# A new order for the second half of a hand-ordered RWKV + FFN kernel, and the last output tile copied out of two PSUM banks

## The chip, the cores and the metric

The kernel runs on one core of one Trainium2 chip. The metric is the device time of one execution in microseconds; lower is better. Each kernel is timed in several runs, and one execution of it is also profiled. The five engines of a core take their instructions in program order, each from its own queue, and wait for each other through semaphores: PE (TensorE, matmuls), DVE (VectorE), ACT (ScalarE), POOL (GpSimd) and SP (SyncE, here only a queue that issues DMAs). Matmuls write PSUM, which has eight banks; DVE and ACT read it from there.

## The reference

A recurrence over 768 tokens for 4 x 8 heads of 48, and behind it a feed-forward block on the 3072 x 384 result:

```python
for t in range(S):
    cur = np.einsum('bhd,bhe->bhde', u[None] * kt, vt)
    y[:, :, t] = np.einsum('bhd,bhde->bhe', rt, state + cur)
    state = wt[:, :, :, None] * state + np.einsum('bhd,bhe->bhde', kt, vt)
...
a = x @ w1
b = x @ w2
h = a * b @ w3
return (h @ w_out).astype(np.float32)
```

x is y with heads side by side (384 columns), d_ff is 1024. Inputs and output are float32.

## The kernel before

The sequence is cut into six chunks of 128 tokens, and chunk and batch into 13 units (`UNITS`): unit t covers one or two batches of one chunk. Units 0 and 1 have one batch, the others two. The state is carried from chunk to chunk; units of the same batches follow each other at a distance of two (5, 7, 9, 11 and 6, 8, 10, 12).

For each unit t the recurrence is written as matmuls. `ln_t` (ACT, L421) takes the logarithm of w, `cs_t` (PE, L437 and L442) sums it up over the tokens into two banks, and ACT reads those banks three times: `pc_t` (L449), `ne_t` (L454, exp of minus the sum) and `e_t` (L495). `iw_t`, `rw_t` (L491), `KRr_t` (L499) and `KRk_t` (L458) scale r and k; `dtr_t` and `dtk_t` (SP, L504 and L519) or `trk_t` with the copy `trke_t` (L529) transpose them. `m_t_b` (PE, L564) is the 128 x 128 product of r and k for batch b, and it is masked either by `msk_t_b` on DVE (L583) or by the copy `mcp_t_b` on ACT (L570) and the masking `maff_t_b` on POOL or DVE. `ys_t` (L599) and `yi_t_b` (L609) sum the output, `rk_t` (L533), `ruk_t` (L537), `dg_t` (L543) and `dv_t` (L552) make the term with u, and `yb_t` (DVE, L627) adds both and so frees the two banks of y. `dty_t_b` (SP, L636) or `yt_t` with `xT_t` transposes the result. `kv_t` (L680, L673), `T_t` (L687, L690), `S_t` (L702) and `Sb_t` (L707) carry the state on.

The feed-forward block of a unit has four groups g: `a_t_g` and `b_t_g` (PE, L727, six matmuls of 128 x 256 each) fill a bank each, `asb_t_g` (ACT, L732) copies a out, `abT_t_g` (DVE, L737) multiplies it with b. `o_t_b` (PE, L748, eight matmuls) multiplies with w34, the product of w3 and w_out that the first half makes (`wt`, `w3Te`, `wm`, `w34e`); `osb_t_b` (L753) copies the 128 x 384 result to one of four buffers, `st_t_b` (L757) stores it. The very last tile, unit 11 batch 0 (`LAST`), is done in two halves of 192 columns, `o_11_0` and `oh_11_0`, each with its own copy and store.

Nothing is scheduled by a compiler. `ORDER` is a list of step@engine in the order of the program; each engine takes its own steps in this order. `BANKS` gives each step its PSUM bank (`y7=3,4`, `cs10=3,4`), its copy of `a_sb` (`sa`), its mask buffer (`M`) and its output buffer (`so`). A step waits for the steps whose data it reads and for the last readers of the bank and buffer that it writes. So with `y7=3,4` and `cs10=3,4` the matmuls of `cs_10` wait until `yb_7` has read the sums of unit 7. No step that reads PSUM is given to POOL.

Of the kernel before, what the change touches and what calls it, by code (L numbers as in the profile page):

```python
# [67 lines left out]
vin_2@POOL warm0@21 cs_0@PE csT_0@PE ne_0@ACT vc_0@ACT KRk_0@DVE w1_1@POOL et_0@ACT ruk_0@DVE warm3@3 trk_0@PE
padet@DVE warm3@3 kv_0@PE trke_0@DVE pc_0@ACT mask@POOL trw_0@PE S_0@DVE KRw_0@DVE ln_2@ACT dg_0@DVE warm3@2 m_0_0@PE
w3_0@POOL Sb_0@ACT msk_0_0@DVE cs_2@PE dv_0@POOL csT_2@PE ne_2@ACT rin_1@POOL yi_0_0@PE et_2@ACT trw_2@PE KRk_2@DVE  # L70
yb_0@DVE w2_1@POOL trk_2@PE ln_1@ACT KRw_2@DVE yt_0@PE trke_2@ACT cs_1@PE w1_0@POOL rk_2@DVE csT_1@PE vin_1@POOL
ruk_2@DVE pc_2@ACT pc_1@ACT ne_1@ACT m_2_0@PE m_2_1@PE dg_2@DVE mcp_2_0@ACT KRk_1@POOL msk_2_1@DVE et_1@ACT
maff_2_0@POOL warm1@4 kv_2@PE xT_0@ACT trk_1@PE trke_1@ACT w2_0@POOL dv_2@DVE yi_2_0@PE yi_2_1@PE win_3@POOL yb_2@DVE
warm7@2 wt_1_0@PE wt_1_1@PE a_0_1@PE wo@POOL w3Te_1@ACT trw_1@PE yt_2@PE asb_0_1@ACT w3_1@POOL KRw_1@DVE wt_0_0@PE
wt_0_1@PE xT_2@DVE m_1_0@PE w3Te_0@DVE kin_3@POOL a_2_2@PE msk_1_0@DVE b_2_2@PE rin_3@POOL asb_2_2@ACT b_0_1@PE
S_2@DVE rk_1@DVE a_2_3@PE abT_0_1@DVE ruk_1@POOL a_0_0@PE abT_2_2@DVE a_2_0@PE dg_1@DVE a_2_1@PE dv_1@POOL asb_2_0@ACT
yi_1_0@PE b_2_0@PE asb_2_1@ACT w3_2@POOL yb_1@DVE kv_1@PE b_2_1@PE w3_3@POOL ln_3@ACT b_2_3@PE win_4@POOL abT_2_1@DVE
asb_2_3@ACT yt_1@PE b_0_0@PE asb_0_0@ACT xT_1@DVE S_1@DVE vin_3@POOL a_1_1@PE abT_2_0@DVE b_1_0@PE abT_2_3@DVE
asb_1_1@ACT b_1_1@PE abT_0_0@DVE cs_3@PE csT_3@PE win_5@POOL ne_3@ACT wm_0@PE et_3@ACT a_1_0@PE pc_3@ACT w34e_0@ACT
wm_1@PE kin_4@POOL asb_1_0@ACT abT_1_0@DVE wt_2_0@PE rin_4@POOL wt_3_0@PE KRk_3@DVE wt_2_1@PE wt_3_1@PE w3Te_2@DVE  # L80
trk_3@PE w3Te_3@ACT abT_1_1@DVE trw_3@PE vin_4@POOL trke_3@ACT Sb_1@DVE wm_2@PE KRw_3@DVE w34e_1@ACT m_3_0@PE
w34e_2@DVE m_3_1@PE wm_3@PE rin_5@POOL msk_3_0@DVE mcp_3_1@ACT maff_3_1@DVE ys_3@PE wt_5_0@PE w34e_3@DVE wt_4_0@PE
wt_4_1@PE kin_5@POOL wt_6_0@PE w3Te_4@DVE wt_6_1@PE wt_5_1@PE wt_7_0@PE w3Te_5@DVE wt_7_1@PE wm_4@PE ln_4@ACT
win_6@POOL rk_3@DVE ruk_3@DVE wm_5@PE w34e_4@ACT dg_3@DVE rin_6@POOL w3Te_6@ACT yi_3_0@PE iw_4@ACT w3Te_7@DVE
yi_3_1@PE cs_4@PE dv_3@DVE kin_6@POOL wm_7@PE e_4@ACT Sb_2@DVE yb_3@DVE ne_4@ACT pc_4@ACT KRk_4@DVE wm_6@PE win_8@POOL
ln_5@ACT yt_3@PE w34e_5@ACT rw_4@DVE trk_4@PE win_9@POOL xT_3@ACT KRr_4@DVE cs_5@PE w34e_7@DVE w34e_6@ACT trr_4@PE
pc_5@ACT trke_4@DVE ne_5@ACT kv_3@PE kv_4@PE T_3@DVE iw_5@ACT o_0_0@PE trre_4@DVE e_5@ACT T_4@DVE m_4_0@PE S_4@POOL
osb_0_0@ACT ys_4@PE msk_4_0@DVE m_4_1@PE st_0_0@SP o_1_0@PE S_3@POOL msk_4_1@DVE win_7@POOL a_3_1@PE ln_6@ACT a_3_2@PE
rk_4@DVE vin_6@POOL asb_3_1@ACT ruk_4@DVE yi_4_0@PE Sb_3@ACT cs_6@PE KRk_5@DVE b_3_1@PE asb_3_2@ACT vin_5@POOL
dg_4@DVE ne_6@ACT csT_6@PE yi_4_1@PE abT_3_1@DVE osb_1_0@ACT trk_5@PE rin_7@POOL et_6@ACT rw_5@DVE a_3_0@PE KRr_5@DVE  # L90
a_3_3@PE trke_5@ACT rin_9@POOL dv_4@DVE b_3_3@PE asb_3_3@ACT KRk_6@DVE trr_5@PE kin_7@POOL pc_6@ACT yb_4@DVE b_3_0@PE
trre_5@ACT trk_6@PE rin_10@POOL rk_6@DVE yt_4@PE abT_3_3@DVE trke_6@ACT b_3_2@PE rin_8@POOL o_2_1@PE xT_4@ACT
abT_3_2@DVE rk_5@DVE asb_3_0@ACT kin_8@POOL m_5_1@PE abT_3_0@DVE m_5_0@PE mcp_5_1@ACT trw_6@PE ruk_5@DVE o_3_1@PE
KRw_6@DVE osb_2_1@ACT maff_5_1@POOL msk_5_0@DVE o_2_0@PE osb_3_1@ACT ruk_6@POOL Sb_4@ACT dg_5@DVE st_3_1@SP m_6_1@PE
osb_2_0@ACT m_6_0@PE msk_6_1@DVE kv_6@PE ln_7@ACT T_6@DVE dv_5@POOL kv_5@PE a_4_2@PE ln_8@ACT b_4_2@PE msk_6_0@DVE
iw_7@ACT vin_8@POOL win_12@POOL o_3_0@PE asb_4_2@ACT T_5@DVE iw_8@ACT vin_7@POOL dg_6@DVE ys_6@PE ys_5@PE yi_5_0@PE
S_5@DVE yi_6_0@PE yi_5_1@PE a_4_1@PE yb_5@DVE yi_6_1@PE dv_6@POOL b_4_1@PE asb_4_1@ACT abT_4_2@DVE osb_3_0@ACT cs_7@PE
abT_4_1@DVE yt_5@PE rw_7@POOL e_7@ACT yb_6@DVE a_4_0@PE b_4_3@PE pc_7@ACT xT_5@DVE asb_4_0@ACT dty_6_0@SP cs_8@PE
ne_7@ACT kin_10@POOL b_4_0@PE ne_8@ACT st_3_0@SP KRk_7@DVE a_4_3@PE KRr_7@DVE e_8@ACT a_5_2@PE KRk_8@DVE dtr_7@SP
ln_9@ACT rk_8@DVE b_5_2@PE ruk_8@POOL b_5_0@PE dty_6_1@SP asb_5_2@ACT pc_8@ACT asb_4_3@ACT a_5_0@PE iw_9@ACT  # L100
abT_5_2@DVE abT_4_3@DVE a_5_1@PE win_10@SP S_6@POOL a_5_3@PE asb_5_0@ACT kin_9@POOL rw_8@DVE asb_5_1@ACT trk_7@PE
abT_4_0@DVE kv_7@PE trke_7@ACT rk_7@DVE b_5_3@PE vin_9@POOL KRr_8@DVE o_4_0@PE Sb_6@ACT Sb_5@ACT abT_5_0@DVE T_7@DVE
asb_5_3@ACT b_5_1@PE S_7@POOL osb_4_0@ACT abT_5_3@DVE m_7_0@PE st_4_0@SP ys_7@PE ruk_7@POOL mcp_7_0@ACT m_7_1@PE
abT_5_1@DVE st_2_1@SP kv_8@PE msk_7_1@DVE st_2_0@SP a_6_2@PE dtk_8@SP cs_9@PE maff_7_0@POOL dg_7@DVE b_6_0@PE ne_9@ACT
dtr_8@SP T_8@DVE a_6_0@PE asb_6_2@ACT KRk_9@DVE e_9@ACT yi_7_0@PE a_6_3@PE rw_9@DVE dtk_9@SP dv_7@DVE asb_6_0@ACT
yi_7_1@PE o_4_1@PE ln_10@ACT rk_10@DVE win_11@SP yb_7@DVE KRr_9@POOL o_5_0@PE osb_4_1@ACT dg_8@DVE Sb_7@ACT pc_9@ACT
asb_6_3@ACT cs_10@PE rk_9@DVE dtr_9@SP yt_7@PE ruk_9@POOL e_10@ACT o_5_1@PE xT_7@DVE st_4_1@SP osb_5_0@DVE pc_10@ACT
# [30 lines left out]
def kernel(  # L138
# [572 lines left out]
    def block(t):  # L711
# [27 lines left out]
        for b in range(nb):  # L739
            row = (b0 + b) * S + c * C  # L740
            parts = 2 if (t, b) == LAST else 1
            for z, mark in enumerate(("", "h")[:parts]):
# [3 lines left out]
                def _(eng, b=b, cols=cols):  # L746
                    for fi in range(FI):
                        nc.tensor.matmul(one(f"o{t}_{b}")[:, cols], lhsT=ab[:, fi, b * C:(b + 1) * C],  # L748
                                         rhs=w34[:, fi, cols], start=(fi == 0), stop=(fi == FI - 1))
# [57 lines left out]
```

## Time and profile before

| | us |
|---|---|
| median of the runs | 164.16 (163.75, 164.16, 164.83) |
| the profiled execution | 163.85 |
| its span, first to last instruction | 162.1 |
| mean granted TensorE clock | 0.997 |

Busy times in the profile are of instructions at work; the time in a semaphore wait is idle, and the view names what ended it. A row of the timeline merges neighbouring instructions of one line; the time of such a piece on a busy PE is best read from its start to the start of the next row, since the ends of matmuls overlap with what follows. On DVE the next instruction of a queue starts about 0.08 us before the end of the one ahead.

### The profile page before, as it was taken

How to read it: one execution, taken by the hardware profiler on the slowest of the kernel's cores; microseconds unless marked ns; L12 is line 12 of the kernel's file. 1: busy time of each engine (PE TensorE's matmuls, PEld its weight loads, DVE VectorE, ACT ScalarE, POOL GpSimd, SP SyncE). 2: the span in 40 equal slices, each digit the busy share in tenths (PEclk: the TensorE clock that was granted, in tenths of full speed). 3: DMA queues.
4: the chain of work that ended last, by engine and by line, in shares of the span. 5: the costliest groups of instructions: out<-in, count | busy, mean ns of one | idle time of the engine just before them, and what ended most of it. 6: DMA issues, size and time to landing. Idle time of an engine off the chain costs nothing.

```text
span 162.1 us, 4606 instructions
## 1 busy us (share of the span) xinstructions
...
## 2 busy tenths in 40 slices
...
GB/s 111 222 159 180 196 195 242 209 170 215 219 155 161 177 259 167 137 120 172 147 186 169 230 202 195 94 142 132 184 174 182 201 28 146 28 121 97 6 146 97
DMA packets 103718, 25.83 MB, mean 159 GB/s; under 512 B 95825, under 2 KB 101713, under 8 KB 103697
## 3 DMA queue, kind: packets, MB, share of 16 engines
...
q10 hardware_dynamic: 144, 0.10, 0.2%
q14 instruction: 7, 0.05, 0.1%
...
## 4 chain that ended last, share of the span: by engine, by line
PE 62%; DMA 20%; POOL 6%; DVE 6%; issue 2%; SPq 1%; ACT 0%; DVEq 0%; POOLq 0%
PE banks L727 31%; PE banks L748 18%; DMA rin<-in_r_dram 9%; DMA w_bf<-in_moe_w_dram 8%; DMA u_f<-in_u_dram 4%; PE banks L564 3%; PE banks L609 2%; PE banks L437 1%; PE banks L680 1%; PE banks L599 1%; PE banks L525 1%; POOL w_bf L358 1%; DVE dg L543 1%; POOL win L343 1%; POOL kin L343 1%
## 5 line engine op out<-in xcount | busy, mean ns | idle before, releaser
L727 PE MATMUL banks<-xT,w_bf 128*128 128x256 bf16 (+1 forms) x624 | 68.6, 264 | 0.0
L727 PEld LDWEIGHTS <-w_bf 128*128 128x128 bf16 x624 | 55.5, 98 | 7.0
L737 DVE TENSOR_TENSOR abT<-a_sb,banks 128x512 bf16<-128x512 f32 x48 | 31.9, 683 | 17.1 <-ACT a_sb L732 9.6
L732 ACT COPY a_sb<-banks 128x512 f32<-128x512 f32 x48 | 27.6, 591 | 21.5 <-PE banks L727 14.7
L748 PE MATMUL banks<-w,abT 128*128 128x384 bf16 (+1 forms) x200 | 33.9, 320 | 0.0
L748 PEld LDWEIGHTS <-abT 128*128 128x128 bf16 x200 | 18.8, 98 | 10.4
L583 DVE TENSOR_TENSOR Mbf<-banks,mask 128x1024 bf16<-128x1024 f32 x14 | 16.9, 1216 | 0.8 <-PE banks L564 0.6
L753 ACT COPY osb<-banks 128x384 f32<-128x384 f32 (+1 forms) x18 | 8.5, 471 | 13.6 <-PE banks L748 11.8
L421 ACT ACTIVATE lw<-win 128x768 bf16<-128x768 f32 (+1 forms) x13 | 10.3, 799 | 10.3 <-DMA win<-in_w_dram 10.3
L343 POOL DMA_DIRECT2D win<-in_w_dram x11 | 12.5, 1140 | 2.8 <-DMA wo_bf<-in_moe_w_out_dram 1.3
L537 POOL TENSOR_TENSOR ruk<-rk,u_bc 128x768 bf16<-128x768 bf16 (+1 forms) x7 | 10.8, 1537 | 4.9 <-DVE rk L533 4.4
L627 DVE TENSOR_TENSOR yb<-banks,dv 128x768 bf16<-128x768 f32 (+1 forms) x13 | 11.6, 892 | 2.4 <-PE banks L609 1.7
L570 ACT CAST Mbf<-banks 128x1024 bf16<-128x1024 f32 x10 | 10.0, 1014 | 4.6 <-PE banks L564 4.5
L454 ACT ACTIVATE NEt<-banks 128x768 bf16<-128x768 f32 (+1 forms) x13 | 9.9, 768 | 3.8 <-PE banks L437 2.7
L343 POOL DMA_DIRECT2D kin<-in_k_dram x8 | 9.1, 1143 | 4.5 <-issue 3.2
L543 DVE TENSOR_REDUCE dg<-ruk 128x16 f32<-128x768 bf16 (+1 forms) x13 | 11.5, 881 | 0.1
L316 PE MATMUL banks<-zeros 128*128 128x512 bf16 x35 | 10.0, 428 | 1.3 <-DVE zeros L257 1.3
L343 POOL DMA_DIRECT2D rin<-in_r_dram x8 | 9.1, 1142 | 2.3 <-PE banks L564 1.4
L343 POOL DMA_DIRECT2D vin<-in_v_dram x8 | 9.1, 1140 | 0.4 <-DMA rin<-in_r_dram 0.4
L564 PE MATMUL banks<-KRT 64*128 64x128 bf16 x192 | 8.1, 217 | 0.4 <-ACT KRT L529 0.3
L609 PEld LDWEIGHTS <-Mbf 128*128 128x128 bf16 x192 | 6.8, 96 | 1.9 <-DVE Mbf L583 0.7
L564 PEld LDWEIGHTS <-KRT 64*128 64x128 bf16 x192 | 5.5, 94 | 3.4 <-issue 1.1
(103 smaller groups left out, 243.6 us busy)
## 6 DMA issues: line engine op xcount, KB each, us to landing
...
```

The source lines that it names most:

```text
L343: QUEUE[eng].dma_start(dst, src)
L421: nc.scalar.activation(LW[:, :, :D], ww, Act.Ln)
L537: vec(eng).tensor_mul(ruks.rearrange("t (b h) d -> t b (h d)", b=nb), rks.rearrange("t (b h) d -> t b (h d)", b=nb), u_bc[:, None, :].to_b ...
L543: nc.vector.reduce_sum(dgs, ruks, axis=AX.X)
L564: nc.tensor.matmul(o[:, e, q, :], lhsT=KRTs[a:a + PAD, 0, b * HP + q, :], rhs=KRTs[a:a + PAD, 1, b * HP + q, :], start=True, stop=True)
L583: nc.vector.tensor_mul(Mbf[bank[f"M{t}_{b}"]], mview(), mask.rearrange("s (j q) t -> s j q t", j=2))
L609: nc.tensor.matmul(o[:, h % 2, b, h // 2, :], lhsT=M[:, h % 2, h // 2, :], rhs=vv[:, b * H + h, :], start=(not c and b == 0 and h < 2), st ...
L627: nc.vector.tensor_add(ybs.rearrange("t b (q e d) -> t e (b q) d", e=2, d=D), yview().rearrange("t e (x d) -> t e x d", d=D), dvs.rearrang ...
L727: nc.tensor.matmul(o[:, f, :], lhsT=wt[:, di, fi * P:(fi + 1) * P], rhs=x[:, di, :T], start=(di == 0), stop=(di == DI - 1))
L732: copier(eng)(a_sb[bank[f"sa{t}_{g}"]], one(f"a{t}_{g}"))
L737: nc.vector.tensor_mul(ab[:, g * per:(g + 1) * per, :T], sa.rearrange("p (f t) -> p f t", t=T), one(f"b{t}_{g}").rearrange("p (f t) -> p f ...
L748: nc.tensor.matmul(one(f"o{t}_{b}")[:, cols], lhsT=ab[:, fi, b * C:(b + 1) * C], rhs=w34[:, fi, cols], start=(fi == 0), stop=(fi == FI - 1))
```

## The change

The order of the first half is kept on every engine. From about unit 7 on (the last third of the list of each engine, 80 us into the span) the order is another one on all five engines, and the banks and buffers there are others. Some steps change engine: to DVE go `trke_7`, `Sb_8`, `osb_7_1`, `osb_8_0`, `osb_12_1` (from ACT) and `KRr_9`, `S_9`, `ruk_11`, `ruk_12` (from POOL); from DVE to POOL go `rw_9`, `S_8`, `KRr_12`, `maff_12_0`; from DVE to ACT `osb_5_0`, `osb_8_1`, `osb_9_0`. The mask of unit 12 batch 1, until now `mcp` on ACT and `maff` on POOL, becomes one `msk` on DVE. In the first half only banks differ: `wt1` goes from 4 to 2, `wt2` from 1 to 2, `a1_0` from 5 to 1, and two runs of idle matmuls (`warm`) go to other banks.

The two halves of the last tile get a bank and an output buffer each (`oh11_0=1 soh11_0=0` beside `o11_0=7 so11_0=1`); before, both had bank 2 and buffer 1.

```diff
-POOL_MASK = {(2, 0), (3, 1), (5, 1), (7, 0), (8, 1), (10, 0), (10, 1), (11, 0), (12, 0), (12, 1)}
+POOL_MASK = {(2, 0), (3, 1), (5, 1), (7, 0), (8, 1), (10, 0), (10, 1), (11, 0), (12, 0)}
...
-M8_0=2 m8_1=0,1 M8_1=0 y8=4,5 kv8=2 a8_0=1 b8_0=4 sa8_0=2 a8_1=7 b8_1=4 sa8_1=1 a8_2=4 b8_2=7 sa8_2=2 a8_3=0 b8_3=3
+M8_0=0 m8_1=1,2 M8_1=2 y8=4,5 kv8=5 a8_0=7 b8_0=2 sa8_0=2 a8_1=3 b8_1=4 sa8_1=0 a8_2=4 b8_2=5 sa8_2=2 a8_3=4 b8_3=5
...
                 @op(f"o{mark}_{t}_{b}")
-                def _(eng, b=b, cols=cols):
+                def _(eng, b=b, cols=cols, mark=mark):
                     for fi in range(FI):
-                        nc.tensor.matmul(one(f"o{t}_{b}")[:, cols], lhsT=ab[:, fi, b * C:(b + 1) * C],
+                        nc.tensor.matmul(one(f"o{mark}{t}_{b}")[:, cols], lhsT=ab[:, fi, b * C:(b + 1) * C],
                                          rhs=w34[:, fi, cols], start=(fi == 0), stop=(fi == FI - 1))
 
                 @op(f"osb{mark}_{t}_{b}")
-                def _(eng, b=b, cols=cols):
-                    copier(eng)(osb[bank[f"so{t}_{b}"]][:, cols], one(f"o{t}_{b}")[:, cols])
+                def _(eng, b=b, cols=cols, mark=mark):
+                    copier(eng)(osb[bank[f"so{mark}{t}_{b}"]][:, cols], one(f"o{mark}{t}_{b}")[:, cols])
```

(`st` takes its buffer in the same way.)

Three places matter below. The first is around `cs_10`, the sum of the logarithms of unit 10. On PE it stood in the list as o_4_1, o_5_0, cs_10, yt_7 with `y7=3,4` and `cs10=3,4`; it now stands as cs_9, o_4_1, o_5_0, yi_7_0, yi_7_1, cs_10, a_6_0, o_5_1, yt_7 with `y7=6,7` and `cs9=1,2`, `cs10=1,2`. On DVE the rows there were these (KR_95 with NEt is `KRk_9`, rw_87 is `rw_9`, dv_109 `dv_7`, rk_102 `rk_10`, yb_111 `yb_7`, dg_106 `dg_8`, rk_103 `rk_9`):

```order
L543 TENSOR_REDUCE dg_107<-ruk_105 128x16
L687 TENSOR_TENSOR Tst_117<-banks,Sst_119 128x384
L458 TENSOR_TENSOR KR_95<-w_bf,NEt_91 128x16x48
L491 TENSOR_TENSOR rw_87<-w_bf,iw_85 128x768
L552 TENSOR_TENSOR dv_109<-vin_73,dg_107 128x768
L533 TENSOR_TENSOR rk_102<-w_bf 128x768
L627 TENSOR_TENSOR yb_111<-banks,dv_109 128x2x8x48
L543 TENSOR_REDUCE dg_106<-ruk_104 128x16
L533 TENSOR_TENSOR rk_103<-w_bf 128x768
```

and are now these (KR_95 with rw_87 is `KRr_9`):

```order
L687 TENSOR_TENSOR Tst_117<-banks,Sst_119 128x384
L543 TENSOR_REDUCE dg_107<-ruk_105 128x16
L552 TENSOR_TENSOR dv_109<-vin_73,dg_107 128x768
L499 TENSOR_TENSOR KR_95<-rw_87,Et_89 128x16x48
L458 TENSOR_TENSOR KR_95<-w_bf,NEt_91 128x16x48
L533 TENSOR_TENSOR rk_102<-w_bf 128x768
L627 TENSOR_TENSOR yb_111<-banks,dv_109 128x2x8x48
L533 TENSOR_TENSOR rk_103<-w_bf 128x768
L543 TENSOR_REDUCE dg_106<-ruk_104 128x16
```

`rk_10` still stands ahead of `yb_7`; `KRr_9` has come over from POOL, where `rw_9` has gone.

The second place is DVE behind `yb_9` (abT_136 is unit 7, abT_129 unit 8, yb_111 `yb_9`). It was this:

```order
L491 TENSOR_TENSOR rw_86<-rin_65,iw_84 128x768
L543 TENSOR_REDUCE dg_106<-ruk_104 128x16
L737 TENSOR_TENSOR abT_136<-a_sb_126,banks 128x512
L627 TENSOR_TENSOR yb_111<-banks,dv_109 128x2x8x48
L737 TENSOR_TENSOR abT_129<-a_sb_128,banks 128x512
L458 TENSOR_TENSOR KR_95<-w_bf,NEt_91 128x16x48
L737 TENSOR_TENSOR abT_129<-a_sb_126,banks 128x512
```

and is now this (`abT_7_2`, `yb_9`, `abT_7_0`, `KRk_11`, `KRr_11`, `S_9`, `Sb_8`, `osb_7_1`, `rw_12`, `abT_8_0`):

```order
L737 TENSOR_TENSOR abT_136<-a_sb_126,banks 128x512
L627 TENSOR_TENSOR yb_111<-banks,dv_109 128x2x8x48
L737 TENSOR_TENSOR abT_136<-a_sb_127,banks 128x512
L458 TENSOR_TENSOR KR_95<-w_bf,NEt_91 128x16x48
L499 TENSOR_TENSOR KR_95<-rw_87,Et_89 128x16x48
L702 TENSOR_TENSOR Sbf_120<-Tst_116,pc_113 128x384
L707 CAST Sbf_121<-Sst_119 128x384
L753 COPY osb_138<-banks 128x384
L491 TENSOR_TENSOR rw_86<-rin_65,iw_84 128x768
L737 TENSOR_TENSOR abT_129<-a_sb_128,banks 128x512
```

Five steps now stand between the last product of unit 7 and `rw_12`. On PE the steps beside them are now b_7_2, cs_12, yi_9_1, a_8_0, a_8_3, a_8_1, o_7_1, kv_10, b_8_3, b_8_0, with `b7_0=2`, `o7_1=2`, `b8_0=2`. On POOL the steps from `KRr_10` on are now KRr_10, dv_9, S_8, dv_10, rw_11, kin_12, KRr_12; they were KRr_10, dv_9, rw_11, kin_12, dv_10, S_9, vin_11.

The third place is the end of ACT's list, here with what each row waits for. Before:

```order
L753 COPY osb_0_137<-banks_61 128x384 [waits DMAHW5_49,PE_49]
L753 COPY osb_3_140<-banks_61 128x384 [waits DMAHW6_49,DVE_49,PE_49]
L753 COPY osb_2_139<-banks_61 128x384 [waits DMAHW7_49,PE_49]
L753 COPY osb_1_138<-banks_61 128x192 [waits DMAHW0_49,DVE_49]
L757 DMA out_0_dram<-osb_1_138 128x192 [waits Activation_49]
```

Now:

```order
L732 COPY a_sb_0_126<-banks_61 128x512 [waits DVE_49,PE_49]
L753 COPY osb_0_137<-banks_61 128x384 [waits DMAHW5_49,PE_49]
L753 COPY osb_2_139<-banks_61 128x384 [waits DMAHW7_49,DVE_49,PE_49]
L753 COPY osb_0_137<-banks_61 128x192 [waits DMAHW1_49,PE_49,Activation_49]
L757 DMA out_0_dram<-osb_0_137 128x192 [waits Activation_49]
```

The last copy, `osbh_11_0`, waited for DVE, whose last copy `osb_11_0` reads the same bank; it now waits for PE itself.

170 lines of the change are left out of this document (85 added, 85 removed).

## The prediction

> **What bounds the kernel now.** I read the stretches first, then the timelines of PE, DVE and POOL around PE's idle time, then the end. Columns of the stretches: stretch, its length, busy time of PE, PEld, DVE, ACT and POOL, granted clock, DMA share, GB/s.
>
> ```profile
> 0.00:20.00 20.00, 15.85 (x158) 8.23 (x158) 15.36 (x34) 10.68 (x19) 17.53 (x24) 1.00 1.42 173
> ...
> 90.00:100.00 10.00, 9.38 (x118) 6.90 (x117) 10.00 (x15) 7.82 (x14) 5.35 (x4) 1.00 1.06 218
> 100.00:110.00 10.00, 10.00 (x158) 8.15 (x153) 9.82 (x15) 7.20 (x11) 8.40 (x8) 1.00 1.80 122
> ...
> 156.00:162.10 6.10, 2.60 (x24) 1.91 (x22) 0.36 (x1) 1.28 (x3) 0.00 (x0) 0.93 0.37 129
> sum 162.10, PE 153.52 PEld 117.34 DVE 125.44 ACT 96.92 POOL 103.16; mean PE 11.81 PEld 9.03 DVE 9.65 ACT 7.46 POOL 7.94
> ```
>
> PE idles 162.10 - 153.52 = 8.58 us: 4.15 in the first 20 us, 3.50 behind its last matmul, 0.62 between 90 and 100, and 0.31 in all the rest. The number of matmuls stays, so a new order can win only what PE waits. The start keeps its order; what is left is the 0.62 and the end. DVE is the second engine: full from 90 to 110.
>
> The one wait of PE in the second half, on PE's and DVE's timeline (start, length, engine, line, tiles):
>
> ```profile
> 92.50 2.76 PE L748 MATMUL banks<-w,abT 128*128 128x384 bf16 x16
> 95.89 0.50 PE L437 MATMUL banks<-lw,LT 128*128 128x384 bf16 x2 [0.62 <-DVE yb L627]
> ...
> 115.89 2.76 PE L748 MATMUL banks<-w,abT 128*128 128x384 bf16 x16
> 118.49 0.82 PE L727 MATMUL banks<-xT,w_bf 128*128 128x256 bf16 x6
> ```
>
> ```profile
> 92.10 0.95 DVE L552 TENSOR_TENSOR dv<-vin,dg 128x768 bf16<-128x768 bf16 x1
> 92.97 2.00 DVE L533 TENSOR_TENSOR rk<-w_bf 128x768 bf16<-128x768 bf16 x1
> 94.89 0.94 DVE L627 TENSOR_TENSOR yb<-banks,dv 128x768 bf16<-128x768 f32 x1
> ...
> 96.61 0.54 DVE L533 TENSOR_TENSOR rk<-w_bf 128x768 bf16<-128x768 bf16 x1
> ```
>
> ```profile
> 92.39 2.15 POOL L499 TENSOR_TENSOR KR<-rw,Et 128x768 bf16<-128x768 bf16 x1 [1.90 <-ACT Et L495]
> ```
>
> The reader sees a chain: `rk_10` took 2.00 where its like takes 0.54, because it stood until POOL's `KRr_9` was done (92.39 + 2.15 = 94.54); behind it `yb_7` came late, and `cs_10`, which takes over yb_7's banks 3,4, waited for it. From o_4_1's start to cs_10's start are 3.39 us, where the same sixteen matmuls elsewhere step on after 118.49 - 115.89 = 2.60. The wait costs 0.79.
>
> The end:
>
> ```profile
> 151.91 6.68 PE L748 MATMUL banks<-w,abT 128*128 128x384 bf16 x48
> ...
> 158.63 0.36 DVE L753 COPY osb<-banks 128x192 f32<-128x192 f32 x1 [4.66 <-PE banks L748]
> 159.03 0.32 ACT L753 COPY osb<-banks 128x192 f32<-128x192 f32 x1 [1.23 <-DVE osb L753]
> ```
>
> PE ends at 158.59, DVE copies one half at 158.63 though its matmuls were over earlier, and ACT copies the other half only behind it, at 159.03.
>
> **The sum, part by part.** *1. cs_10: -0.79.* It now writes banks 1,2, last held by `cs_9`, whose readers are on ACT; `yb_7` no longer holds it. What is late next? Between cs_9 and cs_10 stand two o steps (2.60) and two yi, while ACT needs three short reads of cs_9. `yb_7` itself is next wanted by yt_7, behind cs_10, a_6_0 and o_5_1, some 2.5 us later, against 0.94 for itself. The old hold is gone too: KRr_9 is on DVE now. I take the whole 0.79; bounds 0 and 0.79.
>
> *2. The end: -0.40.* The two halves have two banks. `osb_11_0` can run beside oh_11_0's matmuls, and `osbh_11_0` starts where DVE's copy started, 158.63 in place of 159.03. Its store and what follows move with it. Bounds 0 (if another store ended last) and 0.40.
>
> *3. wt_0 behind wt1: +0.04.* Both now lie in bank 2:
>
> ```profile
> 21.25 1.01 ACT L388 COPY w3T<-banks 128x1024 bf16<-128x1024 bf16 x1 [1.68 <-PE banks L384]
> ...
> 22.28 0.61 PE L384 MATMUL banks<-I,w_bf 128*128 128x128 bf16 x8
> ```
>
> wt_0 must wait for w3Te_1's end, 22.26, plus the 0.06 that PE took from yb_7's end (94.89 + 0.94 = 95.83) to cs_10 (95.89): 22.32 for 22.28.
>
> *4. New order behind unit 7: 0 to +0.4, taken +0.1.* PE and DVE run neck and neck there, so I add up the tightest place, b_7_2 to b_8_0. Rows of DVE by shape (count, busy us, mean ns), and of PE:
>
> ```profile
> L737 DVE TENSOR_TENSOR abT<-a_sb,banks 128x512 bf16<-128x512 f32 x48 | 31.9, 683 | 17.1 <-ACT a_sb L732 9.6 <-PE banks L727 7.3
> L583 DVE TENSOR_TENSOR Mbf<-banks,mask 128x1024 bf16<-128x1024 f32 x14 | 16.9, 1216 | 0.8 <-PE banks L564 0.6
> L627 DVE TENSOR_TENSOR yb<-banks,dv 128x768 bf16<-128x768 f32 x11 | 10.5, 952 | 1.3 <-POOL ruk L537 0.6 <-PE banks L609 0.6
> ...
> L753 DVE COPY osb<-banks 128x384 f32<-128x384 f32 x6 | 3.3, 548 | 0.0
> L499 DVE TENSOR_TENSOR KR<-rw,Et 128x768 bf16<-128x768 bf16 x6 | 3.2, 554 | 0.1
> ...
> L702 DVE TENSOR_TENSOR Sst<-Tst,pc 128x384 f32<-128x384 f32 x2 | 1.1, 549 | 0.0
> ...
> L707 DVE CAST Sbf<-Sst 128x384 bf16<-128x384 f32 x1 | 0.4, 354 | 0.0
> ```
>
> ```profile
> 111.09 0.49 PE L437 MATMUL banks<-lw,LT 128*128 128x384 bf16 x2
> 111.42 0.36 PE L609 MATMUL banks<-wo_bf,Mbf 128*128 128x48 bf16 x8
> 111.62 4.09 PE L727 MATMUL banks<-xT,w_bf 128*128 128x256 bf16 x36
> 115.55 0.50 PE L673 MATMUL banks<-wo_bf,KR 128*128 128x96 bf16 x8
> ...
> 146.67 5.40 PE L727 MATMUL banks<-xT,w_bf 128*128 128x256 bf16 x48
> ```
>
> ```profile
> 151.53 1.94 DVE L737 TENSOR_TENSOR abT<-a_sb,banks 128x512 bf16<-128x512 f32 x3 [2.59 <-PE banks L727]
> ```
>
> A group of six steps on after (115.55 - 111.62) / 6 = 0.655, cs_12 after 0.33, yi after 0.20, kv_10 after 0.34. DVE starts 0.27 behind the group it reads (the seventh of eight groups ends at 146.67 + 7 x 0.655 = 151.26, DVE starts at 151.53). From b_7_2's end, PE can start o_7_1 after 0.33 + 0.20 + 3 x 0.655 = 2.50. DVE has abT_7_0 after 0.27 + 0.68 + 0.87 + 0.60 = 2.42 (each next instruction overlaps by 0.08), with 0.06 to PE 2.48: just in time. Then KRk_11, KRr_11 and S_9 at 0.47 and Sb_8 at 0.27 end at 4.10; osb_7_1 ends at 4.57, PE has it at 4.63. b_8_0, which needs its bank 2, is due at 2.50 + 1.30 + 0.34 + 0.655 = 4.80. Spare: 0.17. S_9 in this form has no row; its neighbour in f32 has 0.549, and POOL's S has 0.82 (quoted below), so its bounds are 0.55 and 0.82; I take the same engine's. Even 0.82 leaves the loss at 0.1. Elsewhere the cover is wider: `msk_12_1`, 1.22 on DVE in place of two steps elsewhere, is ready 0.27 + 0.87 + 1.22 = 2.4 behind yi_11_1, while two o steps, ys_12 and yi_12_0, over 2.8 us of PE, stand ahead of its reader. The other steps that change engine cost nothing by the same reckoning: matmuls cover them. SP's transposes keep their place behind the yb and KR that release them, and stores that are moved past them are short. So: none below 0, since PE has no other wait to lose; up to four places at the limit of this reckoning, 0.1 each, above. I take 0.1, near the lower end, because the place added up came out with time to spare.
>
> Sum against the profiled execution: 163.85 - 0.79 - 0.40 + 0.04 + 0.10 = 162.8. The median of the runs shown, 164.16, lies 0.31 higher; from it the same terms give 163.1. I name 162.9, between the two.
>
> **Rivals.** *A. The ties bite.* Several places with spare times under 0.2 each slip; PE waits a little at each. Against it: spare is positive in the place added up; for it: DVE at 9.82 of 10 in 100:110 has no room to catch up. The upper end of term 4 and a part of term 1 lost give 163.3 to 163.9.
>
> *B. VectorE is held by GpSimd in the tie: slower.* Place: KRk_11, KRr_11 and S_9 behind abT_7_0. POOL's steps ahead:
>
> ```profile
> 105.35 1.63 POOL L499 TENSOR_TENSOR KR<-rw,Et 128x768 bf16<-128x768 bf16 x1 [0.39 <-issue]
> 106.96 1.47 POOL L552 TENSOR_TENSOR dv<-wo_bf,dg 128x768 bf16<-128x768 bf16 x1
> 109.63 1.63 POOL L491 TENSOR_TENSOR rw<-w_bf,iw 128x768 bf16<-128x768 bf16 x1 [1.21 <-ACT iw L487]
> ...
> 114.13 0.82 POOL L702 TENSOR_TENSOR Sbf<-Tst,pc 128x384 bf16<-128x384 f32 x1
> ```
>
> KRr_10, dv_9, S_8, dv_10, rw_11 in a row take 1.63 + 1.47 + 0.82 + 1.47 + 1.63 = 7.02, and from 105.35 end at 112.4. b_7_2 ends at 111.62 + 0.655 - 0.79 - 0.53 (cs_12 and a yi now come behind it) = 110.95, so KRk_11 starts at about 110.95 + 2.42 = 113.4. It decides when POOL is 1.0 us later than that: then a hold of rk_10's size, 2.00 - 0.54 = 1.46, less the 0.17 spare, goes into PE whole: 162.8 + 1.3 = 164.1, slower than 163.85. Against it: rw_10, which releases KRr_10, now comes earlier. The Trainium skill, "SBUF — State Buffer", section "Who interferes with whom", says that a VectorE instruction with two SBUF inputs and a GpSimd instruction that reads SBUF exclude each other, and that the one that comes second blocks until the first is through. By that rule all three steps, with two SBUF inputs each, can be held, and the trace agrees, with 2.00 us for rk_10. It speaks against moving S_9 to VectorE; the sum by it is 164.1 if POOL is late and 162.8 if not.
>
> *C. Transposed tiles land late.* Unit 8's tile was issued from 106.11 and wanted at 112.27:
>
> ```profile
> 106.11 2.49 SPq L636 DMA_TRANSPOSE xT<-yb  x2
> DMA to landing us min/median/max: 4.5/4.9/5.3
> DMA to landing us min/median/max: 2.3/4.7/6.2
> ```
>
> (the second row is of these two, the third of all twelve). The second issue, at 107.35, landed by 111.9, 0.4 ahead of need. Both its release (yb_8) and the need move up by about the same 0.8. At 6.2 it would land 1.3 late: 164.1. Against it: the neighbours on the queue stay.
>
> *D. The end wins nothing*, since a store ends it: 163.2.
>
> **Chances.** My forecast (162.3 to 163.3) 0.58, A 0.18, B 0.09, C 0.06, D 0.04, all else 0.05 (0.02 below, 0.03 above). Range 162.3 to 164.2: it takes in A and the values of B to D and leaves out about 1 in 10. 1% of 164.16, 1.64 us, is about what a measurement of this kernel can tell from no change. Removing both waits whole gives 1.19, so faster by over 1% needs the lower edge of the forecast or a kind scatter of the runs: 0.16. Slower by over 1% needs a hold at several places: 0.05. Within: 0.79.
>
> **What would show it.** Step 1: cs_10 without idle time ahead of it; PE's idle time in 90:100 near 0. Step 2: ACT's last copy within 0.1 us of PE's last matmul, DVE's ended before. Step 3: 0.04 more idle at wt_0. Step 4: PE's idle time between 100 and 155 under 0.4. Rival B: a KR or S row on DVE over 1 us at 112 to 115; C: PE waiting for the DMA of xT. I would be wrong if PE idled elsewhere, above all behind DVE between 97 and 120.

## The result and the profile after

| | before | changed |
|---|---|---|
| median of six runs each, us | 164.14 (163.39 to 165.06) | 162.97 (162.81 to 164.15) |
| ratio, 95% interval | | 0.9934 [0.9905, 0.9962] |
| span of the profiled execution, us | 162.1 | 161.3 |

The gain is 0.7%, and its interval excludes no change, though it is under the 1% that the prediction took as about what a measurement of this kernel can tell from no change. The forecast was 162.9.

The stretches of the changed kernel (columns as before: stretch, length, busy time of PE, PEld, DVE, ACT, POOL, clock, DMA share, GB/s):

```profile
90.00:100.00 10.00, 10.00 (x132) 7.52 (x131) 9.41 (x16) 7.91 (x16) 5.89 (x5) 1.00 1.23 229
100.00:110.00 10.00, 10.00 (x139) 7.90 (x137) 9.81 (x14) 6.67 (x11) 8.68 (x8) 1.00 1.92 129
...
156.00:161.30 5.30, 2.12 (x21) 1.63 (x19) 0.45 (x2) 0.80 (x2) 0.00 (x0) 0.99 0.35 119
```

PE's 0.62 of idle time between 90 and 100 is gone, and no other wait has come in its stead: from 60 to 158 us PE is busy throughout. PE's timeline around `cs_10` in the changed kernel:

```profile
93.70 0.56 PE L609 MATMUL banks<-vin,Mbf 128*128 128x48 bf16 x16
94.11 0.48 PE L437 MATMUL banks<-lw,LT 128*128 128x384 bf16 x2
```

DVE's timeline ahead of `yb_7` there:

```profile
92.50 0.54 DVE L499 TENSOR_TENSOR KR<-rw,Et 128x768 bf16<-128x768 bf16 x1
92.97 0.55 DVE L458 TENSOR_TENSOR KR<-w_bf,NEt 128x768 bf16<-128x768 bf16 x1
93.44 0.55 DVE L533 TENSOR_TENSOR rk<-w_bf 128x768 bf16<-128x768 bf16 x1
94.30 0.96 DVE L627 TENSOR_TENSOR yb<-banks,dv 128x768 bf16<-128x768 f32 x1 [0.32 <-PE banks L609]
```

`cs_10` follows the yi steps at once, 1.15 ahead of the end of `yb_7` (94.30 + 0.96 = 95.26), and `rk_10` takes 0.55 instead of 2.00. The end, all engines:

```profile
155.82 2.30 PE L748 MATMUL banks<-w,abT 128*128 128x384 bf16 x21
...
157.55 0.36 DVE L753 COPY osb<-banks 128x192 f32<-128x192 f32 x1 [1.46 <-PE banks L748]
158.20 0.32 ACT L753 COPY osb<-banks 128x192 f32<-128x192 f32 x1 [0.89 <-PE banks L748]
```

PE ends at 155.82 + 2.30 = 158.12. ACT's last copy starts 0.08 behind it and waits for PE; before, it started 0.44 behind (159.03 against 158.59) and waited for DVE.

Where the gain comes from, in three stretches, with `cs_7` (PE, L437) as a mark near the place where the order begins to differ. In the kernel before it starts here:

```profile
76.26 0.49 PE L437 MATMUL banks<-lw,LT 128*128 128x384 bf16 x2
```

and in the changed kernel here:

```profile
76.58 0.49 PE L437 MATMUL banks<-lw,LT 128*128 128x384 bf16 x2
```

From `cs_7` to PE's last matmul it was 158.59 - 76.26 = 82.33 and is 158.12 - 76.58 = 81.54: 0.79 won. From there to ACT's last copy 0.36 is won. But up to `cs_7` the profiled execution lost 0.32, nearly all of it a stretch in which no engine's order had changed, though some banks had. 0.79 + 0.36 - 0.32 = 0.83, the 159.03 - 158.20 by which the last copy came earlier. The lost 0.32 had no place in the prediction.

### The profile page after: what moved, and what is told of

It is laid out like the page before. It is cut to its first block, busy times and chain, and to the rows that moved or that the text cites. A ratio compares the mean times of both kernels' runs of the same rounds, so it can differ in the third digit from the quotient of the medians.

```text
span 161.3 us, 4596 instructions
## 1 busy us (share of the span) xinstructions
PE 153.0 (95%) x1921; PEld 117.5 (73%) x1923; DVE 125.3 (78%) x204; ACT 93.9 (58%) x158; POOL 101.2 (63%) x95
## 4 chain that ended last, share of the span: by engine, by line
PE 66%; DMA 21%; POOL 6%; DVE 3%; issue 1%; SPq 1%; ACT 0%; DVEq 0%; ACTq 0%; POOLq 0%
PE banks L727 33%; PE banks L748 20%; DMA rin<-in_r_dram 9%; DMA w_bf<-in_moe_w_dram 8%; DMA u_f<-in_u_dram 4%; PE banks L564 3%; PE banks L609 2%; PE banks L680 2%; PE banks L437 1%; PE banks L599 1%; PE banks L525 1%; POOL w_bf L358 1%; POOL win L343 1%; POOL kin L343 1%; POOL Mbf L578 1%
## 5 line engine op out<-in xcount | busy, mean ns | idle before, releaser
L583 DVE TENSOR_TENSOR Mbf<-banks,mask 128x1024 bf16<-128x1024 f32 x15 | 18.2, 1217 | 1.2 <-PE banks L564 1.0
L570 ACT CAST Mbf<-banks 128x1024 bf16<-128x1024 f32 x9 | 9.0, 1013 | 7.8 <-PE banks L564 7.8
L537 POOL TENSOR_TENSOR ruk<-rk,u_bc 128x768 bf16<-128x768 bf16 (+1 forms) x5 | 7.7, 1537 | 6.1 <-DVE rk L533 6.1
L578 POOL TENSOR_SCALAR_AFFINE_SELECT Mbf<-Mbf 128x1024 bf16<-128x1024 bf16 x6 | 6.7, 1115 | 6.7 <-ACT Mbf L570 6.5
L316 PE MATMUL banks<-zeros 128*128 128x512 bf16 x33 | 9.5, 430 | 1.4 <-DVE zeros L257 1.3
L552 POOL TENSOR_TENSOR dv<-vin,dg 128x768 bf16<-128x768 bf16 (+1 forms) x5 | 6.1, 1215 | 3.6 <-DVE dg L543 1.9
```

Source lines behind the costliest of these rows:

```text
L316: nc.tensor.matmul(banks[:, at, :], lhsT=zeros[:, :C], rhs=zeros, start=True, stop=True)
L583: nc.vector.tensor_mul(Mbf[bank[f"M{t}_{b}"]], mview(), mask.rearrange("s (j q) t -> s j q t", j=2))
```

## The experiments

Theory: 0.79 is the wait of `cs_10`, 0.4 the end, and the rest of the new order is worth nothing. Each ratio is against the kernel before, in runs taken beside those of the kernel named. e8, which overwrites data that it still needs, is told at its place.

| kernel | time, us | ratio, 95% interval | span |
|---|---|---|---|
| e1_tail_alone | 163.66 | 0.9973 [0.9948, 0.9998] | 161.7 |
| e2_rk10_behind | 163.52 | 0.9964 [0.9943, 0.9985] | 161.2 |
| e3_both_edits | 162.92 | 0.9936 [0.9913, 0.9959] | 160.8 |
| e4_no_tail | 163.32 | 0.9965 [0.9945, 0.9985] | 161.6 |
| e5_shared_banks | 164.05 | 0.9988 [0.9969, 1.0007] | see there |
| e9_shared_again (one run) | 163.92 | none | 162.2 |
| e6_sb1_act | 163.06 | 0.9935 [0.9911, 0.9959] | 161.3 |
| e7_pool_late | 163.33 | 0.9960 [0.9929, 0.9992] | 161.5 |
| e10_trr4_behind | 163.30 | 0.9946 [0.9930, 0.9961] | 161.9 |
| e11_changed_again | 163.28 | 0.9939 [0.9919, 0.9959] | 161.7 |
| e12_kv3_first | 163.17 | 0.9937 [0.9911, 0.9963] | 161.3 |

### e1 to e4: the two parts, alone and together

e1 is the kernel before with the changed code for the last tile's halves:

```diff
...
+oh11_0=7 soh11_0=0
...
-    copier(eng)(osb[bank[f"so{t}_{b}"]][:, cols], one(f"o{t}_{b}")[:, cols])
+    copier(eng)(osb[bank[f"so{mark}{t}_{b}"]][:, cols], one(f"o{mark}{t}_{b}")[:, cols])
```

> The kernel before, with the last tile's halves in two banks and two buffers and nothing else. My account: ACT's last copy starts within 0.1 us of PE's last matmul in place of 0.44 behind it; the span falls by 0.35 to 0.40 (162.1 to about 161.7), PE still waits 0.6 at cs_10. Rival (another store or the queue ends the kernel): span unchanged within 0.1 although ACT's copy is earlier.

e2 is the kernel before with one step moved on DVE:

```diff
-rk_10@DVE
 yb_7@DVE
+rk_10@DVE
```

> The kernel before, with one step moved: rk_10 behind yb_7 on VectorE, so that its hold by GpSimd's KRr_9 no longer stands ahead of yb_7. My account (that hold made the whole wait): no idle time of PE at cs_10, later work keeps the gain, span 161.3 (0.79 less). Rival (VectorE is full until 114 us and sets the pace, so PE waits a little later instead): PE idles 0.3 us or more between 96 and 120, span 161.6 to 162.1.

e3 makes both edits to the kernel before:

> The kernel before with these two edits together and the old order otherwise. My account (the new order is worth its two places and nothing else): span 160.9 to 161.0, time 162.6 to 163.0, the changed kernel's or 0.3 below. Rival (the rest of the new order carries part of the gain): 163.3 or more.

e4 is the changed kernel with the last tile's halves again in one bank and one buffer:

```diff
...
-oh11_0=1 soh11_0=0
...
-    copier(eng)(osb[bank[f"so{mark}{t}_{b}"]][:, cols], one(f"o{mark}{t}_{b}")[:, cols])
+    copier(eng)(osb[bank[f"so{t}_{b}"]][:, cols], one(f"o{t}_{b}")[:, cols])
```

> The changed kernel with the last tile's halves in one bank and one buffer again. My account: ACT's last copy falls behind VectorE's again, 0.35 to 0.40 us more than the changed kernel: span 161.7, time about 163.3. Rival (the halves' separation is worth nothing in the new order, whose last stores come earlier): span 161.3.

PE's timeline of e1 at `cs_10`:

```profile
95.90 0.50 PE L437 MATMUL banks<-lw,LT 128*128 128x384 bf16 x2 [0.62 <-DVE yb L627]
```

and of e2:

```profile
92.42 2.76 PE L748 MATMUL banks<-w,abT 128*128 128x384 bf16 x16
95.02 0.49 PE L437 MATMUL banks<-lw,LT 128*128 128x384 bf16 x2
```

In e2 `cs_10` comes 2.60 behind o_4_1, the undisturbed step of the prediction. DVE there shows that the hold is still present and only stands elsewhere:

```profile
93.07 0.96 DVE L627 TENSOR_TENSOR yb<-banks,dv 128x768 bf16<-128x768 f32 x1
93.94 0.94 DVE L533 TENSOR_TENSOR rk<-w_bf 128x768 bf16<-128x768 bf16 x1
```

`rk_10` takes 0.94, until POOL's `KRr_9`, which started at 92.31 and took 2.15, is done, but `yb_7` is through ahead of it. The end of e4:

```profile
158.11 0.36 DVE L753 COPY osb<-banks 128x192 f32<-128x192 f32 x1 [2.12 <-PE banks L748]
158.50 0.32 ACT L753 COPY osb<-banks 128x192 f32<-128x192 f32 x1 [1.29 <-DVE osb L753]
```

ACT waits for DVE again and comes 0.39 behind it. From `cs_7` to PE's last matmul it is 82.33 in e1, as in the kernel before, 81.54 in e2 and e3, and 81.53 in e4: moving `rk_10` gives the whole 0.79, and the new order gives the same 81.54. The parts add up in the times too: 0.9973 x 0.9964 = 0.9937, measured 0.9936 together. And e3, two small edits in the old order, gives what the whole new order gives, 0.9934. Apart from these two places, then, the new order neither won nor lost anything that the runs resolve.

### e5 and e9: is it the banks or the hold?

The change does two things at `cs_10`: other banks, and `KRr_9` off POOL, which ends the hold of `rk_10`. e5 puts back only the shared banks:

```diff
-b6_0=7
+b6_0=2
...
-yt7=6
+yt7=1
...
-cs10=1,2
+cs10=6,7
```

> The changed kernel with one thing put back: cs_10 again writes the two banks that y_7 held (6 and 7 here; the transposes of chunk 7's y and the scores b_6_0 go to other banks), so that it cannot start before VectorE's yb_7 has emptied them, while rk_10 still has nothing beside it on GpSimd. In the changed kernel's profile cs_10 starts at 94.11 and yb_7 ends at 94.30 + 0.96 = 95.26. Theory 1 (the separate banks are a cure of their own, beside the removed hold): TensorE idles about 1.15 to 1.2 us at cs_10 with the releaser yb L627, though rk_10 lasts only 0.55; some of it comes back later only if something else waits there, and no such wait is in the changed kernel, so the span is 161.3 + 1.15 = 162.4 (162.0 to 162.6), the ratio against the kernel before about 1.00. Rival (it was the 2.00 us of rk_10 alone, and with it gone the shared banks cost nothing): no idle time at cs_10, span 161.3, ratio 0.993.

The time is the kernel before's again. In the profiled execution TensorE was slow throughout (last section), so that e9 is the same kernel again, for its profile.

> The kernel of e5_shared_banks once more, for a profile: in its first profiled execution TensorE worked at less than half its pace throughout (a projection matmul 511 ns, 264 in the changed kernel), so that no wait could be read. Theory 1: 1.15 to 1.2 us of idle time at cs_10 (L437) with the releaser yb L627, rk_10 at 0.55, span about 162.3. Rival: no wait there, and the 0.9 us by which the timed runs were longer than the changed kernel's lie elsewhere.

DVE's timeline of e9 ahead of `yb_7`:

```profile
93.17 0.55 DVE L533 TENSOR_TENSOR rk<-w_bf 128x768 bf16<-128x768 bf16 x1
94.04 0.96 DVE L627 TENSOR_TENSOR yb<-banks,dv 128x768 bf16<-128x768 f32 x1 [0.32 <-PE banks L609]
```

and PE's at `cs_10`:

```profile
95.06 0.50 PE L437 MATMUL banks<-lw,LT 128*128 128x384 bf16 x2 [1.05 <-DVE yb L627]
```

No hold, and still 1.05 of idle time (1.15 to 1.2 was expected), in the one execution of e9: in the new order `yb_7` waits for the yi steps that now stand just ahead of `cs_10`, so without other banks `cs_10` could only be later. In the old order moving `rk_10` is enough, in the new one the banks are what carries. The last copy starts at 159.15 in e9, and from `cs_7` (76.31) that is 82.84; in the changed kernel it is 158.20 - 76.58 = 81.62. `cs_10` itself is 1.22 later behind `cs_7` (18.75 against 17.53), and the whole of it stays to the end: nothing behind it has slack on PE.

### e7: GpSimd late, rival B put to the test

```diff
 S_8@POOL
+kin_12@POOL
+vin_11@POOL
 dv_10@POOL
 rw_11@POOL
-kin_12@POOL
...
-vin_11@POOL
```

> The changed kernel with GpSimd's two DMA issues kin_12 and vin_11 taken ahead of dv_10 and rw_11, which makes rw_11 about 2.4 us later: it ended at 111.77 and should end at about 114.2, while VectorE's KRk_11 starts at 113.53. Theory 1 (rival B of the prediction, with its condition: GpSimd more than about 1.0 us late): KRk_11 or KRr_11 is held or waits, one of the two rows shows over 1.0 us or VectorE idles there; osb_7_1 comes 0.5 to 0.8 later than 115.25 and, with 0.17 us to spare at b_8_0, TensorE waits 0.3 to 0.6 us at 116; span 161.6 to 161.9, ratio about 0.995 to 0.997. Rival (VectorE has more room there than the sum gave, or TensorE makes it good): no wait of TensorE over 0.1 at 116 us, span 161.3.

DVE's timeline at the place in the changed kernel:

```profile
112.93 0.68 DVE L737 TENSOR_TENSOR abT<-a_sb,banks 128x512 bf16<-128x512 f32 x1
113.53 0.55 DVE L458 TENSOR_TENSOR KR<-w_bf,NEt 128x768 bf16<-128x768 bf16 x1
114.00 0.55 DVE L499 TENSOR_TENSOR KR<-rw,Et 128x768 bf16<-128x768 bf16 x1
114.47 0.55 DVE L702 TENSOR_TENSOR Sbf<-Tst,pc 128x384 bf16<-128x384 f32 x1
114.94 0.35 DVE L707 CAST Sbf<-Sst 128x384 bf16<-128x384 f32 x1
115.25 0.56 DVE L753 COPY osb<-banks 128x384 f32<-128x384 f32 x1
```

and in e7:

```profile
113.60 0.94 DVE L458 TENSOR_TENSOR KR<-w_bf,NEt 128x768 bf16<-128x768 bf16 x1
...
115.68 0.54 DVE L753 COPY osb<-banks 128x384 f32<-128x384 f32 x1
```

with POOL's `rw_11` there:

```profile
112.48 1.64 POOL L491 TENSOR_TENSOR rw<-w_bf,iw 128x768 bf16<-128x768 bf16 x1
```

`KRk_11` was held until 113.60 + 0.94 = 114.54, 0.42 behind POOL's end (114.12), as `rk_10` ended 0.43 behind POOL's `KRr_9` in the kernel before (92.97 + 2.00 against 94.54) and 0.42 in e2 (94.88 against 94.46). The hold costs 0.94 - 0.55 = 0.39, the spare of 0.17 takes its part, and PE should lose 0.22. PE's timeline from o_7_1 to the next o step, first in the changed kernel:

```profile
114.73 0.49 PE L748 MATMUL banks<-w,abT 128*128 128x384 bf16 x2
...
116.70 0.49 PE L748 MATMUL banks<-w,abT 128*128 128x384 bf16 x2
```

and then in e7:

```profile
114.80 0.49 PE L748 MATMUL banks<-w,abT 128*128 128x384 bf16 x2
...
116.92 0.33 PE L748 MATMUL banks<-w,abT 128*128 128x384 bf16 x1
```

It is 1.97 and 2.12: 0.15 lost. The times, 0.9960 against 0.9934 with overlapping intervals, are too coarse for it. The mechanism of rival B is real, and the expectation for e7, 0.3 to 0.6, was too high. With POOL 2.35 later than in the change it costs 0.15, far from the 1.3 of the prediction, because in these rows a hold lasts only as long as POOL's instruction still runs when DVE's begins: `KRk_11` began 0.52 ahead of POOL's end, `rk_10` 1.57. The Trainium skill, "SBUF — State Buffer", section "Who interferes with whom", says that of such a pair the one that comes second blocks until the first is through; both rows agree.

### e6, e8, e10, e11, e12: what sets the first half

The longest wait of PE in the changed kernel's first half behind 20 us is at `m_3_0`. PE's timeline:

```profile
40.43 0.62 PE L564 MATMUL banks<-KRT 64*128 64x128 bf16 x16 [0.35 <-DVE KRT L483]
```

DVE's ahead of it:

```profile
38.83 0.95 DVE L707 CAST Sbf<-Sst 128x192 bf16<-128x192 f32 x1
39.70 0.68 DVE L483 TENSOR_TENSOR KRT<-banks,ETt 128x1024 bf16<-128x1024 bf16 x1
```

and POOL's beside that:

```profile
38.58 1.14 POOL L343 DMA_DIRECT2D vin<-in_v_dram  x1 [0.38 <-issue]
```

The cast `Sb_1` takes 0.95 beside POOL's issue of a load, and `KRw_3`, which `m_3_0` needs, stands behind it. I first took this for the lost 0.32. e6 takes the cast to ACT:

```diff
-Sb_1@DVE
...
 w34e_1@ACT
+Sb_1@ACT
```

> The changed kernel with the cast Sb_1 moved from VectorE to ScalarE, behind w34e_1. Theory 1 (the 0.35 us of TensorE's wait at m_3_0 is Sb_1 held on VectorE for the length of the DMA that GpSimd issues beside it, 0.95 in place of 0.25 us, which makes KRw_3 late): the wait at m_3_0 goes (under 0.05), KRw_3 follows about 0.6 us earlier, and the gain of up to 0.35 is kept as far as the product trr_4, which then waits for KRr_4 and so for the load rin_4; between nothing and 0.35 remains at the end: span 160.95 to 161.3, ratio against the kernel before 0.991 to 0.993. Rival (m_3_0 waits for something else of VectorE's queue and Sb_1's length is a symptom): the wait stays 0.2 or more and the span at 161.3.

The wait at `m_3_0` went, as theory 1 had it, but nothing was won: span 161.3, ratio 0.9935. The gain had gone by `trr_4`, where e6 waits 0.18, and DVE's row of `rw_4` (L491) says why. In the kernel before:

```profile
50.67 0.56 DVE L491 TENSOR_TENSOR rw<-rin,iw 128x768 bf16<-128x768 bf16 x1 [0.60 <-DMA rin<-in_r_dram]
```

in the changed kernel:

```profile
50.99 0.56 DVE L491 TENSOR_TENSOR rw<-rin,iw 128x768 bf16<-128x768 bf16 x1 [0.60 <-DMA rin<-in_r_dram]
```

e11 is the changed kernel a second time:

> The changed kernel itself, beside the two others on the same chip. Theory 1 (the 0.32 us by which its first half was longer in its profile is the landing of rin_4 in that execution, 50.97 against 50.65, and no property of the kernel): cs_7 again 25.6 us after rin_4's landing, with that landing anywhere from 50.5 to 51.1; ratio against the kernel before 0.991 to 0.996. Rival (its first half is longer by construction): cs_7 at 76.5 to 76.6 with rin_4 landing by 50.7.

`rw_4` in e11:

```profile
51.43 0.56 DVE L491 TENSOR_TENSOR rw<-rin,iw 128x768 bf16<-128x768 bf16 x1 [0.59 <-DMA rin<-in_r_dram]
```

and `cs_7` on PE in e11:

```profile
77.01 0.49 PE L437 MATMUL banks<-lw,LT 128*128 128x384 bf16 x2
```

`rw_4` waits for the load of r for unit 4 (`rin_4`), and `KRr_4`, `trr_4` and all that PE does behind them wait for `rw_4`. From its start to that of `cs_7`:

| profiled execution | rw_4 starts | cs_7 starts | between |
|---|---|---|---|
| before | 50.67 | 76.26 | 25.59 |
| changed | 50.99 | 76.58 | 25.59 |
| e1, e2, e3 | 50.69, 50.59, 50.58 | 76.28, 76.17, 76.17 | 25.59, 25.58, 25.59 |
| e4, e6, e7 | 50.89, 51.03, 51.06 | 76.48, 76.61, 76.65 | 25.59, 25.58, 25.59 |
| e9, e11 | 50.73, 51.43 | 76.31, 77.01 | 25.58, 25.58 |
| e10 | 51.56 | 77.26 | 25.70 |
| e12 | 51.08 | 76.58 | 25.50 |

Ten executions with the same order around `trr_4` agree to 0.01, while `rw_4` itself starts anywhere between 50.58 and 51.43. So what PE wins or loses earlier, by a bank or a cast, does not come through as long as PE still has to wait at `trr_4` (e8 below shows the limit); and the lost 0.32 is the start of `rw_4`, 50.99 - 50.67. One kernel alone spreads as far: 50.99 and 51.43 are both the changed one.

The late start can be followed one step further back. The chain that ended last, in the kernel before, runs through these pieces (start, length):

```profile
22.08 12.99 DMA w_bf<-in_moe_w_dram
...
35.37 1.14 POOL kin L343
...
36.72 13.93 DMA rin<-in_r_dram
...
50.67 0.57 DVE rw L491
```

GpSimd waits with `kin_4`, and so with `rin_4` behind it, until an earlier load, a part of w3 (L369), has landed. That load is issued at 22.08 in the kernel before, in the changed one and in e11, and takes 12.99, 13.31 and 13.74; `rin_4` is then issued at 36.72, 37.05 and 37.47 and takes 13.93, 13.92 and 13.93. So the 0.32, and the further 0.44 of e11, arose while the part of w3 was being loaded. In e6 and e7 that load took 12.85 and 12.79, and `rin_4` itself was slower, 14.38 and 14.49. What makes a load slower in one execution than in another stays open.

The rival of e11 in its own terms, `rin_4` landed by 50.7 and `cs_7` late all the same, did not happen; but the landing, 51.40, also lies outside the 50.5 to 51.1 of theory 1. And that the new first half itself makes the loads later is not refuted: in the four profiled executions with the old first half (before, e1, e2, e3) `rw_4` starts at 50.58 to 50.69, in the eight with the new one at 50.73 to 51.56. Against a steady cost of 0.3 speak the timed runs: the spans of e11's twelve executions go from 160.8 to 162.3, those of e3's eleven, with the old first half, from 160.7 to 162.3, and the ratios are 0.9939 and 0.9936. A smaller cost would not show there.

e10 and e12 try to do other work in that wait. e10 (on top of e6):

```diff
-trr_4@PE
 kv_3@PE
-T_3@DVE
 kv_4@PE
+trr_4@PE
 trre_4@DVE
+T_3@DVE
 T_4@DVE
```

> The kernel of e6_sb1_act (Sb_1 on ScalarE) with trr_4 moved behind kv_3 and kv_4 on TensorE, and T_3 behind trre_4 on VectorE. Theory 1 (the pace of the first half is set by the landing of the load rin_4 through rw_4, KRr_4 and trr_4: in seven profiled executions, of the kernel before, of the changed one and of e1, e2, e3, e4 and e6, cs_7 starts 25.60 to 25.62 us after it, wherever TensorE stood before): with kv_3 and kv_4 (0.6 us) done while KRr_4 is awaited, cs_7 comes less than 25.5 us after the landing, 25.2 to 25.3 if nothing binds next, and 0.1 to 0.4 us of it stays at the end: span 160.9 to 161.2, time 162.6 to 162.9, ratio against the kernel before 0.989 to 0.992. Rival (the constant distance comes from a place further on, which waits for a later load of the same queue): cs_7 stays 25.6 us after rin_4's landing, the idle time moves to that place, and span and time are the changed kernel's.

e12 (on top of e6):

```diff
 w34e_6@ACT
-w34e_7@DVE
+w34e_7@ACT
...
-trr_4@PE
 kv_3@PE
+trr_4@PE
```

> The kernel of e6_sb1_act with kv_3 alone moved ahead of trr_4 on TensorE, and the cast w34e_7 moved from VectorE to ScalarE, which takes 0.47 us out of VectorE's row KRr_4, w34e_7, trke_4, T_3, trre_4, T_4. Ten profiled executions show cs_7 25.58 to 25.59 us behind the start of rw_4, which waits for the load rin_4; in e10, where kv_3 and kv_4 stood ahead of trr_4, m_4_0 came 0.11 earlier behind rw_4, and the matmuls of ys_4 then waited for T_4, whose bank they take. Theory 1 (the pace is rin_4's landing through trr_4, and e10 gave its gain back at T_4): kv_3 (0.31) fills the wait at trr_4, T_4 ends about 3.3 us behind rw_4's start in place of 3.9, and cs_7 starts 25.3 to 25.45 us behind rw_4; where rin_4 lands still differs between executions, so the time falls by no more than 0.1 to 0.3 us against the changed kernel: ratio against the kernel before 0.990 to 0.994. Rival (another place further on sets the distance): cs_7 stays 25.58 us behind rw_4 and the ratio is the changed kernel's 0.994.

In e10 `m_4_0` starts 3.68 behind `rw_4` (55.24 against 51.56), 0.11 sooner than in the changed kernel (54.78 - 50.99 = 3.79), and then it is lost again. PE's timeline of e10:

```profile
55.24 0.40 PE L564 MATMUL banks<-KRT 64*128 64x128 bf16 x8
55.47 0.60 PE L599 MATMUL banks<-Sbf,KRT 64*128 64x48 bf16 x16
```

and DVE's:

```profile
54.65 1.01 DVE L687 TENSOR_TENSOR Tst<-banks,Sst 128x384 f32<-128x384 f32 x2
```

`ys_4` (L599) takes 0.60, 0.36 in the changed kernel: it writes the banks of `kv_3` and `kv_4`, and `T_3` and `T_4`, which now follow each other behind `trre_4`, read them until 54.65 + 1.01 = 55.66. In e12, where `T_3` keeps its place, the distance is 25.50, 0.09 less than in the ten and short of the expected 25.3 to 25.45. In the time that is too little to see: 0.9937, against 0.9939 for e11. So the distance does hang on this place, but only 0.1 of it was had by these moves, and no kernel here is faster than the changed one by more than the runs resolve. Loading `rin_4` earlier was not tried; the load just ahead of it, k of unit 4, has a reader that waits for it as well, `KRk_4`, 0.35 in e12.

e8 was meant to separate the new banks of the first half from the place of `Sb_1`:

```diff
-wt1=2
+wt1=4
...
-wt2=2
+wt2=1
...
-a1_0=1
+a1_0=5
...
-warm4@4
+warm1@4
...
-warm2@2
+warm7@2
```

> The changed kernel with the banks of the first half as before (first transposes of chunks 1 and 2 in banks 4 and 1, a_1_0 in bank 5, the warming products' banks). Theory 1 (the 0.32 us that the first half took longer in the changed kernel's profile came from how the cast Sb_1 fell beside a DMA issue, which no bank sets and which differs between executions): cs_7 starts anywhere from 76.1 to 76.6, its place goes with the length of Sb_1 (0.25 to 0.95), and the time is the changed kernel's within 0.2 us. Rival (the shared bank 2 of the first two chunks' transposes costs it): wt_0's wait for w3Te_1 (0.03) goes, cs_7 starts by 76.2 whatever Sb_1's length is, and the time falls by 0.3 us to about 162.65, ratio 0.991.

It does not separate them. In the changed list `wt_1_0` stands ahead of `trke_1`, so that with the old bank 4 the transposed weights overwrite the transposed k of unit 1 before it is copied; and PE gets two waits that neither kernel has, 0.67 at 21 us and 0.47 at 39 us (163.75 us, ratio 0.9985 [0.9955, 1.0015]). Bank and place in the list go together. But e8 shows where the wait for `rin_4` stops covering what PE loses. The load lands early there, at 50.2, and PE comes late; PE's timeline, the last row of `cs_5` and `trr_4`:

```profile
52.55 0.34 PE L442 MATMUL banks<-ones_c,lw 128*128 128x1 bf16 x8
52.76 0.61 PE L510 MATMUL banks<-I,KR 128*128 128x128 bf16 x8
```

From the one start to the other it is 0.21, without a wait; in the changed kernel it is 0.47 (51.73 to 52.20), in the kernel before 0.40 (51.48 to 51.88), in e1 0.25. So the cover that PE has at `trr_4` was 0.26, 0.19 and 0.04 (read from start to start; the view counts less of it as idle, since the ends of matmuls overlap). What PE loses ahead of it beyond that does reach the end: `cs_7` starts at 77.12 in e8, 0.54 later than in the changed kernel, though the load came 0.8 earlier.

## Why the prediction was right

*Step 1, -0.79, held to the hundredth*: 82.33 to 81.54 between `cs_7` and PE's last matmul. In the changed kernel this is the sum of steps 1 and 4; e2 and e3, where step 4 does not enter, show the same 0.79. Of its two reasons, other banks and the hold gone, e9 shows that the second alone would not have done in the new order.

*Step 2, -0.40, measured -0.36*, and e4 and e1 show it on either side: ACT's last copy starts 0.08 behind PE's last matmul in e1 and 0.49 behind it in e4. The 0.04 is that ACT starts 0.08 behind PE's last matmul, where DVE started 0.04 behind it.

*Step 3, +0.04, is the term that was wrongly put.* The shared bank costs what the step said. ACT's `w3Te_1` in the changed kernel:

```profile
20.97 1.01 ACT L388 COPY w3T<-banks 128x1024 bf16<-128x1024 bf16 x1 [1.39 <-PE banks L384]
```

and `wt_0` on PE:

```profile
22.03 0.61 PE L384 MATMUL banks<-I,w_bf 128*128 128x128 bf16 x8
```

It starts 0.05 behind the copy's end, 21.98. But neither this nor the 0.35 at `m_3_0` reached the end in the changed kernel: PE still waited at `trr_4`. The step counted a cost on PE in a stretch whose end is set by a load, with 0.19 to spare in the kernel before; the row that says so, `rw_4` waiting 0.60 for the DMA, was in the profile of before, and the prediction did not read it. It did no harm because the term was small. The 0.32 by which the profiled first half came out longer is that load's landing, for which the prediction had no term: it took the first half as fixed because its order is. Whether the change has a part in it stays open.

*Step 4, 0 to +0.4, taken +0.1, measured 0.* The only wait of PE behind 41 us, 0.13 of idle time ahead of `trr_4`, lies in the first half, and e3, without the new order, takes the same 81.54 behind `cs_7`. The place added up came out as reckoned: `osb_7_1` ended at 115.25 + 0.56 = 115.81, with 0.17 to spare by the same sum, and e7 spent that spare and 0.15 more.

*The rivals.* A is refuted with step 4. B did not happen, `rw_11` being over at 111.77, 1.8 ahead of `KRk_11`; e7 shows that its price of 1.3 was too high even with its condition met. C did not happen, no wait for xT shows. D is refuted by e1: its last copy starts 82.41 behind `cs_7` (158.69 - 76.28), 0.36 less than the 82.77 of before, and its time fell by 0.27%, about 0.4.

*The sum.* 163.85 - 0.79 - 0.36 + 0.32 = 163.02, where the changed kernel's profiled execution took 162.96. That the forecast of 162.9 fits so closely owes something to chance: it lay 0.1 above the sum of its terms, steps 2, 3 and 4 together came out 0.1 better than put, and the 0.32 of the load, which no term foresaw, went the other way. How early `rw_4` was in the timed executions is not known, since only one of them has a trace.
